# Attention over pooled keys, then an MLP: a waiting matmul group moved ahead of the keys' turn, a pooling sum moved from GpSimd to VectorE, and a transpose and three loads moved in time

## The chip, the cores and the metric

One Trainium2 chip; the program uses one core of it. The metric is the device time of one execution in microseconds. The kernel before took 284.84 us, the median of 3 runs (284.4 to 284.98).

## The reference

Shapes: q, k and v are [8, 8, 576, 64] (batch B, head, row, head size D) in float32, w_in is [512, 2048], w_out is [2048, 512].

```python
k_p = k.reshape(B, H, Sp, 8, D).mean(axis=3)      # Sp = 72 pooled keys
v_p = v.reshape(B, H, Sp, 8, D).mean(axis=3)
scores = scale * np.matmul(q, k_p.transpose(0, 1, 3, 2))
attn = softmax(scores)                             # with 1e-9 in the denominator
x = np.matmul(attn, v_p)                           # heads side by side: [4608, 512]
h = x @ w_in
out = (h - np.tanh(h)) @ w_out                     # [4608, 512]
```

Keys and values are pooled in eights, so that attention is small; the two matrix products of the MLP are most of the work.

## The kernel before

**Groups.** The 4608 rows are cut into nine groups of 512. Group b (0 to 7) holds the first 512 rows of batch b; the 64 left-over rows of every batch make up group 8, which runs last. The inputs of group 8 collect in the tile `xT_last`. Each group has an h stage (x times w_in, tanh, subtraction: `mlp_h` for group 0, L605; `h_pair`, L638, for the others) and an out stage (`mlp_o`, L611, for group 0; `product`, L683, for the others). Attention of the next batch is put between the matmuls of the out stage. The order of all instructions is written by hand: each engine runs its own in program order, and waits where it needs another engine's result or a free buffer.

**The out stage of group 0** (L1018 to L1083) is where the change lies. `mlp_o(0, tb, qd)` is four matmuls of 512 columns: row block tb (0 to 3), quarter qd of the hidden size. Quarter 0 needs the w_out rows of `w2_dmas[0]`, quarter 1 those of `w2_dmas[1]`, quarter 2 those of `w2_dmas[2]`, quarter 3 those of `w2_dmas[3]` (the loads `load_w2(0, 4)`, `(8, 4)`, `(4, 4)`, `(12, 4)`, L835 to L918). These loads turn float32 into float16 on their way and are issued by GpSimd; they run behind the loads of w_in, and on the same queue lie two loads of values of batch 1 (the second is `v1_last`, L917). Results go to PSUM banks 0 to 3.

**Batch 1 in that stage.** `pool_k(1, nc.gpsimd, last=nc.vector)` (L1018) adds eight rows of keys to one in three steps: 8 to 4 rows (L261), 4 to 2 (L267), 2 to 1 (L270, result `kd`). The first two run on GpSimd, the third, because of `last`, on VectorE. Behind it VectorE copies the queries of batch 1 from 16-bit storage (`q_bf`, L1020). `k_transpose(1)` (L360) turns `kd` on TensorE with five matmuls against the identity; VectorE copies the result out of PSUM with L342, L343 and L346 into `KB`. `q_pe_transpose` (L223) does the same for queries, four matmuls per pair of heads, copied out by ScalarE (L144). These, the scores (`scores_wide`, L406) and what follows take PSUM banks 4, 5, 6, 7 in turn (`ps_b1` over `Banks(4, 5, 6, 7)`, L1005): the keys' turn gets 4 and 5, query pairs 0 and 1 get 6 and 7, pairs 2 and 3 get 4 and 5 again. `pool_v1` (L300) sums the values of batch 1 on VectorE, tiles 2 and 3 of them after `v1_last` has landed. `av(1, blk)` (L540) makes block blk of x: matmuls L487, then on VectorE a reciprocal (L522) and a product (L523) into `x_sb`. `turn1(blk)` transposes it on TensorE (L566), and ScalarE copies it to `xT` (L573).

**Sums of weights.** The groups after 0 use sums and differences of quarters of w_out (`sum0` to `sum3`, L1006 to L1016, all by `w_sum`, L670, on VectorE with both inputs in SBUF). `sum1(4)` and `sum0(4)` (L1056, L1057) stand on VectorE between the products of `av(1, 1)` and `av(1, 2)`; `sum0(4)` reads the rows of `w2_dmas[3]`.

**Loads of batch 2.** `load_k(2)`, `load_v(2)`, `load_q(2)` (L1051 to L1053) are issued by SyncE, whose queue also carries every DMA transpose and the stores of group 0. `after(load_k(2), v1_last)` makes SyncE wait with them until `v1_last` has landed. When the keys of batch 2 have landed, GpSimd pools them (`pool_k(2, nc.gpsimd)`, L1077): L261 in two pieces of two and three tiles (`halves`), then L267 and L270.

**The left-over x of batch 0.** `av(0, 4)` (L995) writes it into the tile `x_end`, and `x_dma_transpose(0, 2)` (L996) has SyncE transpose it by DMA into `xT_last` (L557). The tile `P` holds the other blocks of x of batch 0 in `P[:, 0:4, :]` (L117), and is later written by `sum_p` (L651) in the h stage of group 1.

Of the kernel before, what the change touches and what calls it, by code (L numbers as in the profile page):

```python
# [43 lines left out]
def kernel(  # L44
# [57 lines left out]
    P = const.tile([128, NP, TG], BF16, name="P")  # L102
# [46 lines left out]
    def load_main(src, dst, b, t0, t1, eng=nc.sync):  # L149
        return eng.dma_start(out=dst[:, t0:t1, :], in_=src[b, 0:128, t0:t1, :])  # L150
# [7 lines left out]
    def load_dense(src, dst, b, eng=nc.sync):  # L158
        return eng.dma_start(
            out=dst[0 : NM * LO, NM, :], in_=src[b, 128:PR, :, :]  # L160
        )

    def load_k(b, eng=nc.sync):
        return [
            load_main(k_pairs, k_raw[b % 2], b, 0, NM, eng),
            load_dense(k_pairs, k_raw[b % 2], b, eng),
        ]
# [7 lines left out]
    def load_q_tail(b, t, eng):  # L175
        eng.dma_start(
            out=t[:QT, :, R, :], in_=q[b, :, QA:S, :].rearrange("h p d -> p h d")
        )

    def load_q(b, tail=True):  # L180
        if b not in q_raws:
            q_raws[b] = raw.tile([128, H, R + 1, D], FP32, name="q_raw", tag="q_raw")
        t = q_raws[b]
        nc.sync.dma_start(
            out=t[:, :, 0:R, :], in_=q[b, :, 0:QA, :].rearrange("h (p j) d -> p h j d", j=R)
        )
        if tail:
            load_q_tail(b, t, nc.sync)
# [62 lines left out]
    def halves(n, b):  # L251
        return ((0, n),) if b < 2 else ((0, n // 2), (n // 2, n))

    def pool_k(b, eng, t0=0, t1=NT, last=None):
        r = k_raw[b % 2].rearrange("p t (j d) -> p t j d", d=D)[:, t0:t1, :, :]
        if b not in kdups:
            kdups[b] = work.tile([128, NT, 2, D], BF16, name="kd", tag="kd", bufs=1)
        kd = kdups[b][:, t0:t1, :, :]
        n = t1 - t0
        for ta, tb in halves(n, b):  # L260
            eng.tensor_tensor(  # L261
                out=r[:, ta:tb, 0:4, :],
                in0=r[:, ta:tb, 0:4, :],
                in1=r[:, ta:tb, 4:8, :],
                op=ALU.add,
            )
        eng.tensor_tensor(  # L267
            out=r[:, :, 0:2, :], in0=r[:, :, 0:2, :], in1=r[:, :, 2:4, :], op=ALU.add
        )
        kd_done = (last or eng).tensor_tensor(  # L270
            out=kd,
            in0=r[:, :, 0:1, :].to_broadcast([128, n, 2, D]),
            in1=r[:, :, 1:2, :].to_broadcast([128, n, 2, D]),
            op=ALU.add,
        )
        return kd_done
# [63 lines left out]
    def kb_main(kb, ps, t0, t1, engs):  # L340
        kv = kb.rearrange("p (t x) -> p t x", x=KP)
        engs[0](out=kv[0:D, t0:t1, 0:G], in_=ps[0:D, :, 0:G])  # L342
        engs[1](out=kv[D:128, t0:t1, G:128], in_=ps[D:128, :, G:128])  # L343

    def kb_left(kb, ps, eng):
        eng(  # L346
            out=kb[D:128, :].rearrange("p (t x) -> p t x", x=KP)[:, :, 128 : 128 + LO],
            in_=ps[D:128, 0 : NM * LO].rearrange("p (x t) -> p t x", t=NM),
        )

    def turn_tile(dst, kd, t):
        nc.tensor.matmul(
            dst,
            lhsT=kd[:, t, :, :].rearrange("p a d -> p (a d)"),
            rhs=ident[:, :],
            start=True,
            stop=True,
        )

    def k_transpose(b, alloc, engs=(nc.vector.tensor_copy, nc.scalar.copy)):  # L360
        kd = kdups.pop(b)
        ps = alloc([128, NM, 128], FP32, "kT_ps")
        for t in range(NM):
            turn_tile(ps[:, t, :], kd, t)
        kb_main(KB[b % 2], ps, 0, NM, engs)
        ps = alloc([128, 128], FP32, "kT_ps")
        turn_tile(ps[:, :], kd, NM)
        kb_left(KB[b % 2], ps, nc.vector.tensor_copy)
# [131 lines left out]
    def av_half(b, blk, half, x_sb, alloc):  # L500
        ps = alloc([128, 4, D1], FP32, "x_ps")
        av_mms(b, blk, half, ps)
        rden = work.tile([128, 4, 1], FP32, name="rden", tag="rden", bufs=4)
        nc.vector.reciprocal(out=rden[:, :, :], in_=ps[:, :, D:D1])
        nc.vector.tensor_tensor(
            out=x_sb[:, half, :, :],
            in0=ps[:, :, 0:D],
            in1=rden[:, :, :].to_broadcast([128, 4, D]),
            op=ALU.mult,
        )  # L510

    def av_both(b, blk, x_sb):
        b0 = ps_a.ids[ps_a.n % len(ps_a.ids)]
        ps_a.n += 2
        ps = PS[:, b0 : b0 + 2, 0 : 4 * D1].rearrange("p k (h d) -> p k h d", d=D1)
        if b < 2:
            for half in range(2):
                av_mms(b, blk, half, ps[:, half, :, :])
        else:
            head_av_mms(b, blk, ps)  # L520
        rden = work.tile([128, 2, 4, 1], FP32, name="rden2", tag="rden2")
        nc.vector.reciprocal(out=rden[:, :, :, :], in_=ps[:, :, :, D:D1])  # L522
        nc.vector.tensor_tensor(  # L523
            out=x_sb[:, :, :, :],
            in0=ps[:, :, :, 0:D],
            in1=rden[:, :, :, :].to_broadcast([128, 2, 4, D]),
            op=ALU.mult,
        )

    x_pairs = {}  # L530

    def x_block(b, blk):
        if blk == 4:
            x_pairs[b, 2] = work.tile([128, 2, 4, D], BF16, name="x_end", tag="x_end", bufs=1)
            return x_pairs[b, 2]
        if blk % 2 == 0:
            x_pairs[b, blk // 2] = work.tile([128, 2, 2, 4, D], BF16, name="x_sb", tag="x_sb")
        return x_pairs[b, blk // 2][:, blk % 2]

    def av(b, blk, alloc, both):  # L540
        x_sb = x_block(b, blk)
        if both:
            av_both(b, blk, x_sb)
        else:
            for half in range(2):
                av_half(b, blk, half, x_sb, alloc)
        return x_sb

    def x_dma_transpose(b, n):
        if n < 2:  # L550
            nc.sync.dma_start_transpose(
                out=xT[b % 2][:, 2 * n : 2 * n + 2, :, :].rearrange("p k f c -> p (k f) c"),
                in_=x_pairs.pop((b, n)).rearrange("p k a h d -> p (k a h d)"),
            )
        else:
            c = (b % 2) * QT
            nc.sync.dma_start_transpose(  # L557
                out=xT_last[:, b // 2, :, c : c + QT],
                in_=x_pairs.pop((b, 2))[128 - QT : 128].rearrange("p a h d -> p (a h d)"),
            )  # L560
# [44 lines left out]
    def mlp_h(g, i, gts, pool):  # L605
        mlp_h_mms(g, i, 0, NFB, pool)
        mlp_h_act(i, gts)
# [3 lines left out]
    def mlp_o(g, tb, qd, gts):  # L611
        if qd == 0:
            o_tiles[tb] = bank((1, 2, 3, 0)[tb], [128, DM])
        o_ps = o_tiles[tb]
        i0 = W2_ORDER[qd]
        for i in range(i0, i0 + 4):
            nc.tensor.matmul(  # L617
                o_ps[:, :],
                lhsT=gts[i][:, tb * 128 : (tb + 1) * 128],
                rhs=w2b[:, i, :],  # L620
                start=(i == 0),
                stop=(i == NHID - 1),
            )
        if qd == 3:
            nc.scalar.copy(out=O[:, tb, :], in_=o_ps[:, :])
# [127 lines left out]
    w2_dmas = []  # L753
# [13 lines left out]
    def after(lds, dep):  # L767
        for ld in lds:
            tc.add_manual_dep(
                ld.ins,  # L770
                dep.ins.name,
                mybir.DependencyInfo(mybir.DependencyClass.Sync, mybir.DependencyReason.DATA),
            )
# [143 lines left out]
    v1_last = load_main(v_pairs, v_raw[1], 1, 2, 4, nc.gpsimd)  # L917
    load_w2(12, 4)  # L918
    gts = []
# [67 lines left out]
    for i in range(5, NHID):  # L987
        mlp_h(0, i, gts, bank(i % 5 if i > 5 else 5, [128, TG]))
        if i == 7:
            q_pe_tail(0)  # L990
        if i == 9:
            scores_tail(0)
        if i == 11:
            ps_a.n = 0
            av(0, 4, ps_any, True)  # L995
            x_dma_transpose(0, 2)  # L996
    def turn1(blk):
        x_pe_transpose(1, blk, x_pairs[1, blk // 2][:, blk % 2])

# [24 lines left out]
    mlp_o(0, 0, 0, gts)  # L1024
    mlp_o(0, 1, 0, gts)
    mlp_o(0, 2, 0, gts)
    k_transpose(1, ps_any, (nc.vector.tensor_copy, nc.vector.tensor_copy))
    q_pe_transpose(1, (0, 1), "act")
    mlp_o(0, 3, 0, gts)
    sum1(0)  # L1030
    sum2(0)
    sum0(0)
# [15 lines left out]
    mlp_o(0, 1, 2, gts)  # L1048
    mlp_o(0, 2, 2, gts)
    ps_a.n = 0  # L1050
    after(load_k(2), v1_last)  # L1051
    load_v(2)
    load_q(2)  # L1053
    av(1, 0, ps_any, True)
    av(1, 1, ps_any, True)
    sum1(4)  # L1056
# [131 lines left out]
```

## Time and profile before

| what | value |
|---|---|
| median of the runs | 284.84 us |
| the profiled execution's own time | 284.74 us |
| its span, first to last instruction | 282.9 us |
| busy: TensorE / VectorE / ScalarE / GpSimd | 274.3 / 222.6 / 155.2 / 118.5 us |
| h stage of group 1 begins (first matmul of L630) | 52.67 us |
| moved by DMA | 49.82 MB, mean 176 GB/s |

The span begins with the first instruction. A time such as "35.65" is microseconds from there. In a row of the timeline the first number is the start, the second the length; rows of equal kind are merged and counted (x4), and the brackets give the engine's idle time ahead of the row and what ended it. PE is TensorE, PEld its weight loads, DVE VectorE, ACT ScalarE, POOL GpSimd, SP SyncE. Matmul rows contain the pipeline's depth: a matmul of 512 columns is listed with 379 ns, while the next starts some 216 ns after it. A DMA's time to landing runs from its issue to its completion.

### The profile page before, as it was taken

To read this page: it belongs to the slowest core of one execution; us is meant where nothing else is said; L and a number is where in the kernel's file an instruction comes from. 1 tells how busy PE (TensorE), PEld (TensorE's weight loads), DVE (VectorE), ACT (ScalarE), POOL (GpSimd) and SP (SyncE) were. 2 spreads that over 40 slices of the span, in tenths; PEclk is the share of its full clock that TensorE was granted. 3 is DMA by queue.
4 is the path that set the end of the run, shared out by engine and by line. 5 is a ranking of instruction groups with operands and counts; after the bars stand their busy time and mean duration, and the time that the engine had idled before them with its cause. 6 is when DMAs were issued, how large, how long until landed. Compare 5 with 4: busy or idle time off the path is not lost.

```text
span 282.9 us, 5497 instructions
## 1 busy us (share of the span) xinstructions
PE 274.3 (97%) x2174; PEld 180.8 (64%) x2174; DVE 222.6 (79%) x336; ACT 155.2 (55%) x209; POOL 118.5 (42%) x132
## 2 busy tenths in 40 slices
PE   7999899999999999999999999999999999999994
PEld 3574355645974588458944895489547954884583
DVE  6658687999957996699759985999599749936983
ACT  4767373697337653766276628571867056216610
POOL 8844601992596039802980199019900200010000
PEclk9999999999999999999999999999999999999999
DMA  7999998999958894779588949796640440011014
GB/s 250 237 212 270 231 229 256 333 203 256 273 94 214 240 289 88 181 253 331 89 177 267 324 76 156 235 340 123 134 143 1 80 154 2 0 73 79 0 39 111
DMA packets 66491, 49.82 MB, mean 176 GB/s; under 512 B 42104, under 2 KB 55944, under 8 KB 66466
## 3 DMA queue, kind: packets, MB, share of 16 engines
q1 hardware_dynamic: 55538, 33.87, 47.5%
q0 software_dynamic: 8736, 13.77, 20.1%
q10 hardware_dynamic: 2192, 1.84, 2.2%
q8 instruction: 17, 0.28, 0.4%
q14 instruction: 8, 0.07, 0.1%
HBM read 36.70 MB, written 9.44 MB: 163 GB/s over the span
## 4 chain that ended last, share of the span: by engine, by line
PE 83%; DMA 10%; POOL 3%; DVE 1%; issue 1%; SPq 0%; POOLq 0%; DVEq 0%
PE PS L630 39%; PE PS L687 33%; DMA w1b<-in_moe_w_in_dram 5%; PE PS L617 4%; DMA k_raw<-in_k_dram 3%; PE PS L446 3%; PE PS L472 2%; DMA xT<-x_sb 2%; POOL k_raw L261 1%; DVE x_sb L523 1%; PE PS L487 1%; POOL v_raw L827 1%; POOL k_raw L267 1%; PE PS L398 1%; PE PS L566 0%
## 5 line engine op out<-in xcount | busy, mean ns | idle before, releaser
L630 PE MATMUL PS<-xT,w1b 128*128 128x512 bf16 (+1 forms) x504 | 98.1, 355 | 0.5 <-DMA xT<-x_sb 0.5
L644 DVE TENSOR_TENSOR Gt<-PS,TS 128x1024 bf16<-128x1024 f32 x56 | 68.3, 1220 | 32.1 <-ACT TS L643 32.1
L630 PEld LDWEIGHTS <-w1b 128*128 128x128 f16 x576 | 56.4, 98 | 53.5 <-issue 0.7
L643 ACT ACTIVATE TS<-PS 128x1024 f32<-128x1024 f32 x56 | 57.3, 1024 | 30.3 <-PE PS L630 28.2
L731 POOL TENSOR_TENSOR m<-O,m 128x512 f32<-128x512 f32 x6 | 7.6, 1260 | 75.6 <-ACT m L729 62.2
L687 PE MATMUL PS<-w2s,Dg 128*128 128x256 f16 x256 | 30.2, 272 | 0.0
L261 POOL TENSOR_TENSOR k_raw<-k_raw 128x512 f32<-128x512 f32 (+2 forms) x13 | 21.3, 1651 | 17.6 <-DMA k_raw<-in_k_dram 17.6
L467 ACT ACTIVATE E<-PS 72x1024 bf16<-72x1024 f32 (+1 forms) x30 | 26.0, 929 | 4.0 <-PE PS L446 3.7
L687 PEld LDWEIGHTS <-Gt 128*128 128x128 bf16 x256 | 23.6, 98 | 6.8 <-issue 2.3
L687 PEld LDWEIGHTS <-P 128*128 128x128 bf16 x256 | 24.5, 98 | 3.0
L687 PEld LDWEIGHTS <-Dg 128*128 128x128 bf16 x256 | 24.6, 98 | 2.8
L652 DVE TENSOR_TENSOR P<-Gt 128x1024 bf16<-128x1024 bf16 x32 | 22.0, 686 | 0.5
L703 POOL DMA_DIRECT2D out_dram<-O x14 | 7.7, 554 | 31.7 <-DVE O L741 29.5
L738 ACT COPY m<-PS 128x512 f32<-128x512 f32 x8 | 4.7, 585 | 29.6 <-PE PS L687 29.6
L662 DVE TENSOR_TENSOR Dg<-Gt 128x1024 bf16<-128x1024 bf16 x32 | 20.4, 682 | 0.0
L523 DVE TENSOR_TENSOR x_sb<-PS,rden 128x512 bf16<-128x512 f32 x28 | 19.4, 691 | 1.0
L282 POOL TENSOR_TENSOR v_raw<-v_raw 128x512 f32<-128x512 f32 (+1 forms) x12 | 19.2, 1616 | 0.0
L687 PE MATMUL PS<-w2s,Gt 128*128 128x256 f16 x128 | 16.4, 273 | 0.0
L687 PE MATMUL PS<-w2b,P 128*128 128x256 f16 x128 | 16.3, 273 | 0.0
L687 PE MATMUL PS<-w2b,Gt 128*128 128x256 f16 x128 | 16.3, 272 | 0.0
L687 PE MATMUL PS<-w2s,Q 128*128 128x256 f16 x128 | 16.3, 272 | 0.0
L1150 ACT COPY O<-PS 128x512 f32<-128x512 f32 x7 | 4.1, 585 | 21.9 <-PE PS L687 21.9
(123 smaller groups left out, 400.5 us busy)
## 6 DMA issues: line engine op xcount, KB each, us to landing
k_raw<-in_k_dram SPq DMA_DIRECT2D x7, 1024.0 KB, 6.1
out_dram<-O POOLq DMA_DIRECT2D x14, 512.0 KB, 4.4
v_raw<-in_v_dram SPq DMA_DIRECT2D x6, 1024.0 KB, 8.1
q_raw<-in_q_dram SPq DMA_DIRECT2D x6, 1024.0 KB, 11.4
w1b<-in_moe_w_in_dram POOLq DMA_DIRECT2D x4, 512.0 KB, 13.9
w2b<-in_moe_w_out_dram POOLq DMA_DIRECT2D x4, 512.0 KB, 21.6
v_raw<-in_v_dram POOLq DMA_DIRECT2D x2, 512.0 KB, 21.9
out_dram<-O SPq DMA_DIRECT2D x2, 512.0 KB, 6.3
```

Source lines behind the costliest of these rows:

```text
L261: eng.tensor_tensor(out=r[:, ta:tb, 0:4, :], in0=r[:, ta:tb, 0:4, :], in1=r[:, ta:tb, 4:8, :], op=ALU.add,)
L282: eng.tensor_tensor(out=r[:, ta:tb, 0:4, :], in0=r[:, ta:tb, 0:4, :], in1=r[:, ta:tb, 4:8, :], op=ALU.add,)
L446: nc.tensor.matmul(dst, lhsT=kv[a * D : (a + 1) * D, m, :], rhs=rhs, start=True, stop=True,)
L467: nc.scalar.activation(out=e, in_=ps, func=ACT.Exp, scale=SCALE)
L523: nc.vector.tensor_tensor(out=x_sb[:, :, :, :], in0=ps[:, :, :, 0:D], in1=rden[:, :, :, :].to_broadcast([128, 2, 4, D]), op=ALU.mult,)
L617: nc.tensor.matmul(o_ps[:, :], lhsT=gts[i][:, tb * 128 : (tb + 1) * 128], rhs=w2b[:, i, :], start=(i == 0), stop=(i == NHID - 1),)
L630: nc.tensor.matmul(dst[:, t0 * 128 : t1 * 128], lhsT=w1b[:, fb, i * 128 : (i + 1) * 128], rhs=x[:, t0:t1, fb, :], start=(fb == 0), stop=(f ...
L643: nc.scalar.activation(out=t2, in_=PS[:, b0 : b0 + 2, :], func=ACT.Tanh)
L644: nc.vector.tensor_sub(out=Gt[:, p, :, :], in0=PS[:, b0 : b0 + 2, :], in1=t2)
L652: nc.vector.tensor_tensor(out=P[:, a:b, :], in0=Gt[:, a:b, 0, :], in1=Gt[:, a:b, 1, :], op=ALU.add)
L662: return nc.vector.tensor_tensor(out=Dg[:, a:b, :, :], in0=Gt[:, a:b, :, 0:HT], in1=Gt[:, a:b, :, HT:TG], op=ALU.subtract,)
L687: nc.tensor.matmul(part(g, bk, tt), lhsT=lhs(k, slice(tt * 128, (tt + 1) * 128)), rhs=rhs[:, k, :], start=(first and k == 0 and (tt == 0 o ...
```

## The change

Five edits, all in or near the out stage of group 0:

1. In `pool_k`, the second sum (L267) also goes to the engine given as `last`. Only the call for batch 1 gives one, so that there VectorE does the second and the third sum, and GpSimd the first alone.
2. `mlp_o(0, 3, 0)` is moved from behind `q_pe_transpose(1, (0, 1))` to ahead of `k_transpose(1)`.
3. The left-over x of batch 0 is put into `P[:, 4, :]` instead of the tile `x_end`.
4. `x_dma_transpose(0, 2)` is moved from behind `av(0, 4)` to behind `load_q(2)` in SyncE's queue.
5. `load_k(2)` waits for `w2_dmas[2]` instead of `v1_last`; `load_v(2)` and `load_q(2)` follow it in the same queue.

```diff
         (pool_k)
-        eng.tensor_tensor(
+        (last or eng).tensor_tensor(
             out=r[:, :, 0:2, :], in0=r[:, :, 0:2, :], in1=r[:, :, 2:4, :], op=ALU.add
         )
...
     def x_block(b, blk):
+        if b == 0:
+            x_pairs[b, 2] = P[:, 4, :].rearrange("p (s h d) -> p s h d", s=2, h=4)
+            return x_pairs[b, 2]
...
             av(0, 4, ps_any, True)
-            x_dma_transpose(0, 2)
...
     mlp_o(0, 2, 0, gts)
+    mlp_o(0, 3, 0, gts)
     k_transpose(1, ps_any, (nc.vector.tensor_copy, nc.vector.tensor_copy))
     q_pe_transpose(1, (0, 1), "act")
-    mlp_o(0, 3, 0, gts)
...
     ps_a.n = 0
-    after(load_k(2), v1_last)
+    after(load_k(2), w2_dmas[2])
     load_v(2)
     load_q(2)
+    x_dma_transpose(0, 2)
     av(1, 0, ps_any, True)
     av(1, 1, ps_any, True)
```

## The prediction

> **What bounds the kernel now.** First the page's busy times and the shares of the chain that ended last:
>
> ```profile
> PE 274.3 (97%) x2174; PEld 180.8 (64%) x2174; DVE 222.6 (79%) x336; ACT 155.2 (55%) x209; POOL 118.5 (42%) x132
> ...
> PE 83%; DMA 10%; POOL 3%; DVE 1%; issue 1%; SPq 0%; POOLq 0%; DVEq 0%
> ```
>
> TensorE has 8.6 us without work in a span of 282.9, so an edit pays only where TensorE stands. The waits between 28 and 68 us show one place in the change's reach; here is that stretch in TensorE's timeline, then the chain of waits behind it:
>
> ```profile
> 31.48 2.75 PE L617 MATMUL PS<-w2b,Gt 128*128 128x512 f16 x12
> 35.65 0.45 PE L352 MATMUL PS<-ident,kd 128*128 128x128 bf16 x5 [1.41 <-DVE kd L270]
> 35.98 0.62 PE L228 MATMUL PS<-ident,q_bf 128*128 128x128 bf16 x8
> 36.44 1.03 PE L617 MATMUL PS<-w2b,Gt 128*128 128x512 f16 x4
> 37.30 0.61 PE L228 MATMUL PS<-ident,q_bf 128*128 128x128 bf16 x8
> ```
>
> ```profile
> 20.24 9.84 DMA k_raw<-in_k_dram
> 30.22 2.91 POOL k_raw L261
> 33.20 1.53 POOL k_raw L267
> 34.76 0.84 DVE kd L270
> 35.65 0.45 PE PS L352 x5
> ```
>
> The fourth L617 group (36.44) waits for nothing, yet stands behind the keys' turn. Matmuls of 512 columns issue 0.216 us apart, so TensorE could go on at 34.07, and stands 1.58 us in issue time (1.41 by listed ends).
>
> Two more views limit what can be won. DMAs to landing, for `w2_dmas[1]` (issued 12.62), `w2_dmas[2]` (20.04), `v1_last` (23.11), `w2_dmas[3]` (25.82):
>
> ```profile
> w2b<-in_moe_w_out_dram POOLq DMA_DIRECT2D x1, 512.0 KB, 25.5
> ...
> w2b<-in_moe_w_out_dram POOLq DMA_DIRECT2D x1, 512.0 KB, 21.6
> ...
> v_raw<-in_v_dram POOLq DMA_DIRECT2D x1, 512.0 KB, 19.9
> ...
> w2b<-in_moe_w_out_dram POOLq DMA_DIRECT2D x1, 512.0 KB, 19.7
> ```
>
> They land at 38.1, 41.6, 43.0 and 45.5. The first user of `w2_dmas[1]` starts at 38.20 where it could at 38.08: TensorE is already 0.12 us ahead of the weights. And GpSimd against VectorE:
>
> ```profile
> 48.72 3.24 POOL L261 TENSOR_TENSOR k_raw<-k_raw 128x512 f32<-128x512 f32 x2 [13.99 <-DMA k_raw<-in_k_dram]
> 52.04 1.87 POOL L267 TENSOR_TENSOR k_raw<-k_raw 128x640 f32<-128x640 f32 x1
> ```
>
> ```profile
> 47.78 1.28 DVE L670 TENSOR_TENSOR w2s<-w2b 128x1024 f16<-128x1024 f16 x2
> ...
> 51.08 1.43 DVE L670 TENSOR_TENSOR w2s<-w2b 128x1024 f16<-128x1024 f16 x1
> ...
> 53.27 1.19 DVE L670 TENSOR_TENSOR w2s<-w2b 128x1024 f16<-128x1024 f16 x1
> ```
>
> A weight sum takes 0.68 us, but 1.43 and 1.19 beside GpSimd. Both end 0.55 us after GpSimd's instruction of the moment (51.96 and 53.91): VectorE waits out the whole instruction. The pair at 47.78 (`sum1(4)`, `sum0(4)`) escapes, because GpSimd comes only at 48.72.
>
> [...] the products L523 (one input in PSUM) keep 0.69 us beside GpSimd. [...] the trace's 128x640 sum L270 has 826.
>
> **The change part by part.** The sum is against the profiled execution: 282.9 span plus 1.84 around it, 284.74; the median is 284.84.
>
> *Second sum on VectorE.* GpSimd loses L267 (1.52 us). VectorE gains one of 640 float32 elements: 0.83. VectorE's last subtraction ends at 33.00, GpSimd's first sum at 33.12, so the new sum runs 33.16 to 33.99, and `kd` is ready at 34.86 instead of 35.59: 0.73 sooner. Nothing new waits behind it: the copies L1020 stood behind the same wait. They follow 0.73 sooner (their queries came 21.7 us after 11.74, at 33.4).
>
> *`mlp_o(0, 3, 0)` ahead.* Same four matmuls, 4 x 0.216 = 0.86, from 34.07 to 34.93. Its bank's last reader ended at 33.00. `kd` comes at 34.86 plus 0.06 handover: the wait is gone, almost to the point. Either edit alone would leave some: 0.73 or 0.86 of 1.58.
> What is late next: the matmuls were cover for banks. Turn and first queries take 0.79 us as before, to 35.72. Queries 2 and 3 need bank 4, read by L342 and L343: VectorE is free at 35.45, 0.45 + 0.40 later it is 36.31, plus 0.06. TensorE waits 0.65 us, to 36.37. Then 0.45 + 0.11 + 0.22 (from the starts 37.30, 37.75, 37.86) to 37.15 for the first quarter-1 matmul, against 38.20.
> Gain 1.58 - 0.65 + 0.12 = **1.05 us**, if the weights have landed by 37.15. Scores and their exponentials after that find banks free (ScalarE's copies of queries end by about 38.2).
>
> *Transpose moved.* Its issue (1.28 us of SyncE at 30.07) leaves, and so does its traffic at 34 to 37.6. The table by microsecond from 34 (last columns: clock, DMA share, GB/s):
>
> ```profile
> 35.00:36.00 1.00, 0.35 (x6) 0.30 (x7) 1.00 (x3) 0.00 (x0) 0.00 (x0) 1.00 1.25 87
> 36.00:37.00 1.00, 1.00 (x13) 0.73 (x12) 0.99 (x4) 0.58 (x2) 0.00 (x0) 1.00 0.96 207
> ...
> 38.00:39.00 1.00, 1.00 (x6) 0.38 (x4) 0.81 (x2) 1.00 (x4) 0.00 (x0) 1.00 1.26 222
> ```
>
> In 35 to 36 the weights' queue starts 29 packets, in 38 to 39 it starts 199, and 93 in 36 to 37: (170 + 106)/199 = 1.4 us lost; a little is the mixture of packet sizes. I take 1.2 (bounds: 0, if the stall has another cause, and 2.3: `w2_dmas[1]` came 4.7 us after the load ahead of it, its fellow `w2_dmas[3]` 2.5 after `v1_last`, and the difference also holds other traffic). So all later landings come 1.2 sooner: 36.9, 40.4, 41.8, 44.3. That meets 37.15, and `v1_last`'s values are in `VB` 1.94 later, at 43.8, before `av(1, 0)` at 44.43.
> In its new place it goes past the six load issues on SyncE and stands ahead of the store, issued at 50.91, that waits for ScalarE: SyncE idles there from 46.7. Its packets run behind the queries' loads, which landed at 57.0 and now come sooner. The new reader of `P[:, 4, :]` must be done before the sum that rewrites it, past 64 us; behind that sum stand the subtractions L644, but there are some 8 us of slack. Cost 0. Writing to `P` instead of `x_end` costs 0: same product, 0.69 us, no user there.
>
> *Loads sooner.* Batch 2 loads issue at 40.4 instead of 43.0. Their first packets came 1.9 us after the issue, so at 42.3, when the weights' last packets are still due. Before, the keys met that tail too (0.2 us of it); [...] the keys land not 2.6 but about 1.2 sooner: 48.5 to 47.3, and GpSimd's first sum wants to start at 48.72 - 1.2 = **47.5**. `w2_dmas[3]` [...] from 44.3 at worst to 45.9; its user comes at 47.32 - 1.05 = 46.27. Cost 0 (0 to 0.3).
>
> *The point that decides.* `sum1(4)` and `sum0(4)` now start at 46.73 and 47.33 (1.05 sooner). GpSimd at 47.5 comes just after the second has started, and waits for it, as before. Then the rest keeps its pattern, and from 51.62 on TensorE's rows simply move. The 0.48 us wait for `xT` at 83.09 stays.
> Sum: 284.74 - 1.05 = **283.69**.
>
> **Rivals.**
> *A, as above:* 283.7 (283.2 to 284.2).
> *B, GpSimd gets in between the two sums* (start 46.73 to 47.33, keys 0.2 to 0.8 us sooner than I take): `sum0(4)` waits for the first piece of L261 (1.26 us, fastest row): ends 1.13 later. The reciprocal and product of `av(1, 2)` stand behind it, and `turn1(2)` on TensorE has no slack (its input was just in time). Net +0.08: 284.8.
> *C, slower:* GpSimd starts ahead of `sum1(4)`, that is before 46.73, from keys 2.0 us sooner on. With 46.4: first piece to 47.66, `sum1(4)` to 48.21, second piece (1.80) to about 49.95, `sum0(4)` to 50.5 instead of 48.0. `turn1(2)` stands 2.4 us: net +1.35, 286.1. For it: the loads are issued 2.6 us sooner, and the bound of 2.3. Against it: the tail of the weights.
> *D, the weights come no sooner* (the stall isn't the transpose's): quarter 1 waits to 38.1, and the gain is 0.1: 284.6. For it: the transpose moves only 64 KB (64 rows of 512 values of 2 bytes). Against it: the stall lies inside their time.
>
> **Numbers.** A 0.55, B 0.14, C 0.21, D 0.10. The likeliest gives 283.7. The range starts at 283.2, and reaches past D and B to 285.8, into C's lower part; about 2 in 10 is left out. Cases of both signs: A's own range is 283.2 to 284.2. A measurement of this kernel tells about 0.2% (0.57 us) from no change. Faster: A and a little of D, 0.57; same: B and the rest of D, 0.21; slower: C, 0.22.
>
> **What would show it.** L352 starts near 34.95 with no wait for `kd`, and a new wait of 0.65 stands before the second L228 group. Quarter 1 starts near 37.15; near 38.1 is D. The table has no slice near 87 GB/s around 35. `sum1(4)` and `sum0(4)` with 0.68 each are A; one of them over 1.2 is B or C, with an L566 row behind a wait for L523. The h stage of group 1 starts at 51.6 (A), 52.7 (B), 54.0 (C). I am wrong if the stall of 35 to 36.3 is not the transpose's, or if the keys' landing moves with their issue.

## The result, and the profile after

The kernel after took 286.13 us, the median of 18 runs (284.55 to 288.01). The kernel before, in runs taken between them on the same chip, took 284.72 us (18 runs). The ratio is 1.0065 [1.0041, 1.0088] (in brackets here and below: the 95% interval): the change makes the kernel slower, by 0.65%, where the forecast was 1.05 us (0.37%) faster. Ratios compare mean times and leave out three single slow runs (291.42 us of before here, 287.92 and 289.60 us in the third and fourth experiment); the medians here lie 0.50% apart. The time lies outside the range, 0.3 us above its end, and the case that came true is C. The profiled execution took 287.29 us, with a span of 285.6.

The page after, busy times and shares of the chain that ended last:

```profile
PE 275.4 (96%) x2172; PEld 181.8 (64%) x2174; DVE 226.4 (79%) x337; ACT 155.6 (54%) x209; POOL 117.6 (41%) x131
...
PE 89%; DVE 4%; DMA 4%; issue 1%; POOL 1%; DVEq 0%; POOLq 0%
```

DMA's share of the chain fell from 10% to 4% and GpSimd's from 3% to 1%, as intended: the long chain of loads and sums behind `kd` is gone. VectorE's share rose from 1% to 4%; the two weight sums of the new wait are 1.3 points of it (3.66 us), the rest is spread over many short pieces. TensorE's idle time went from 8.6 us of the span to 10.2. TensorE's timeline after shows the old wait gone and the new one there (line numbers past the edits are three higher: L617 is now L620, L566 is L569, L630 is L633, L670 is L673):

```profile
31.61 3.62 PE L620 MATMUL PS<-w2b,Gt 128*128 128x512 f16 x16
35.06 0.44 PE L352 MATMUL PS<-ident,kd 128*128 128x128 bf16 x5
...
36.40 0.61 PE L228 MATMUL PS<-ident,q_bf 128*128 128x128 bf16 x8 [0.45 <-DVE KB L343]
...
37.17 1.03 PE L620 MATMUL PS<-w2b,Gt 128*128 128x512 f16 x4
...
51.39 0.40 PE L569 MATMUL PS<-ident,x_sb 128*128 128x128 bf16 x4 [2.30 <-DVE x_sb L523]
```

Up to 37.17 everything stands where the forecast put it. The second sum takes 0.81 us on VectorE (L267 at 33.05); the forecast's 0.83 is what the sum L270 of the same 128x640 took before, 826 ns. Sixteen matmuls run through, the keys' turn starts at 35.06 with no wait (forecast 34.95), a wait for bank 4 takes its place, and quarter 1 starts at 37.17 (forecast 37.15, before 38.20). Then, at 51.39, 2.30 us are lost for the product of `av(1, 2)`. The chain of waits after tells what was in front of that product:

```profile
46.84 3.66 DVE w2s L673 x2
...
50.64 0.70 DVE x_sb L523
51.35 0.05 issue
51.39 0.40 PE PS L569 x4
```

The two weight sums `sum1(4)` and `sum0(4)`, 1.28 us together before, take 3.74 us, and 3.66 of that is on the path. VectorE's timeline after lists the pair, and GpSimd's names the reason:

```profile
46.75 3.74 DVE L673 TENSOR_TENSOR w2s<-w2b 128x1024 f16<-128x1024 f16 x2
```

```profile
46.46 3.48 POOL L261 TENSOR_TENSOR k_raw<-k_raw 128x512 f32<-128x512 f32 x2 [14.51 <-DMA k_raw<-in_k_dram]
```

GpSimd's first sum starts at 46.46, 2.26 us sooner than before (48.72), and 0.29 us ahead of `sum1(4)` (46.75). One by one: GpSimd's pieces run from 46.46 to 47.73 and from 47.69 to 49.94; `sum1(4)` ends at 48.27, `sum0(4)` at 50.49, each about 0.55 us after a piece. This is the pattern of case C.

GpSimd came so soon because its keys did. DMAs to landing after, for `w2_dmas[1]` (issued at 12.87), `v1_last` (22.66), `w2_dmas[3]` (26.44) and the keys of batch 2 (39.61):

```profile
w2b<-in_moe_w_out_dram POOLq DMA_DIRECT2D x1, 512.0 KB, 22.9
...
v_raw<-in_v_dram POOLq DMA_DIRECT2D x1, 512.0 KB, 18.1
...
w2b<-in_moe_w_out_dram POOLq DMA_DIRECT2D x1, 512.0 KB, 16.8
...
k_raw<-in_k_dram SPq DMA_DIRECT2D x1, 1024.0 KB, 6.7
```

They land at 35.8, 40.8, 43.3 and 46.3. Each is 2.2 to 2.4 us sooner than in the first profile of before, where the forecast took 1.2.

A second loss shows only in the table by microsecond after (the third number from the end is TensorE's granted clock):

```profile
52.00:53.00 1.00, 1.00 (x10) 0.70 (x8) 1.00 (x2) 0.72 (x2) 1.00 (x1) 0.77 2.00 190
53.00:54.00 1.00, 1.00 (x9) 0.73 (x8) 1.00 (x2) 0.76 (x2) 1.00 (x2) 0.50 0.58 66
...
56.00:57.00 1.00, 1.00 (x11) 0.89 (x10) 1.00 (x1) 0.06 (x1) 1.00 (x1) 1.00 0.38 82
```

From 52.5 on, after the wait, TensorE runs at half its clock for some 3.4 us. That costs up to 1.7 us (an estimate, half of 3.4): the h stage of group 1 begins at 55.23, where case C said 54.0. Of the 18 runs, 7 took 287.29 to 288.01 us, with a mean clock of 0.990 to 0.993 over the run; the other 11 took 284.55 to 286.28, with 0.996 to 1.0. The medians of the two sets, 287.70 and 285.95, lie 1.75 apart.

### The profile page after: what moved, and what is told of

The parts are those of the page before. It is cut to its first block, busy times and chain, and to the rows that moved or that the text cites. A ratio compares the mean times of both kernels' runs of the same rounds, so it can differ in the third digit from the quotient of the medians.

```text
span 285.6 us, 5496 instructions
## 1 busy us (share of the span) xinstructions
PE 275.4 (96%) x2172; PEld 181.8 (64%) x2174; DVE 226.4 (79%) x337; ACT 155.6 (54%) x209; POOL 117.6 (41%) x131
## 4 chain that ended last, share of the span: by engine, by line
PE 89%; DVE 4%; DMA 4%; issue 1%; POOL 1%; DVEq 0%; POOLq 0%
PE PS L633 39%; PE PS L690 33%; PE PS L591 5%; PE PS L620 4%; PE PS L446 3%; PE PS L472 2%; DMA v_raw<-in_v_dram 2%; DMA xT<-x_sb 2%; DVE x_sb L523 1%; DVE w2s L673 1%; PE PS L398 1%; PE PS L487 1%; PE PS L877 0%; DVE rden L522 0%; PE PS L944 0%
## 5 line engine op out<-in xcount | busy, mean ns | idle before, releaser
L633 PE MATMUL PS<-xT,w1b 128*128 128x512 bf16 (+1 forms) x504 | 98.5, 356 | 0.1
L633 PEld LDWEIGHTS <-w1b 128*128 128x128 f16 x576 | 56.6, 98 | 53.6 <-issue 0.8
L620 PE MATMUL PS<-w2b,Gt 128*128 128x512 f16 x64 | 16.2, 395 | 0.0
```

Source lines behind the costliest of these rows:

```text
L620: nc.tensor.matmul(o_ps[:, :], lhsT=gts[i][:, tb * 128 : (tb + 1) * 128], rhs=w2b[:, i, :], start=(i == 0), stop=(i == NHID - 1),)
L633: nc.tensor.matmul(dst[:, t0 * 128 : t1 * 128], lhsT=w1b[:, fb, i * 128 : (i + 1) * 128], rhs=x[:, t0:t1, fb, :], start=(fb == 0), stop=(f ...
```

## The experiments

**The theories.** *Lock:* GpSimd's sooner start on the keys of batch 2 makes both weight sums wait, and that is the loss. *Rival, keys' side:* the rewrite around the keys' turn (edits 1 and 2) costs elsewhere. *Rival, loads:* the earlier loads delay others. Each kernel below was run beside the kernel before, whose median was 284.47 for the first four experiments (75 runs), 284.36 for the next four (35 runs) and 284.12 for the last three (35 runs).

### The two sums moved to where GpSimd is idle

```diff
     (the kernel after; new place: right behind pool_v1(2, 4))
+    sum1(4)
+    sum0(4)
...
     av(1, 1, ps_any, True)
-    sum1(4)
-    sum0(4)
```

> The changed kernel, with sum1(4) and sum0(4) moved ahead of av(1, 0) on VectorE, where it stood idle from 42.8 to 45.1 us; nothing else. Lock theory (the two sums wait out GpSimd's first sums of keys, and TensorE's 2.3 us wait for x_sb of block 2 comes from that): the wait is gone, the h stage of group 1 starts at 51.6 instead of 55.2, no slice of the clock at half, 283.6 us, 1.1 below the kernel before. Rival 1 (the sooner loads themselves cost the time, by contention among transfers): the wait stays within 0.5 us of its size, 286. Rival 2 (the clock drop has another cause): the wait goes, but runs still split in two groups 1.7 us apart.

Measured: 284.19 us (283.55 to 284.56, 22 runs), ratio to before 0.9987 [0.9972, 1.0002]. VectorE's timeline of this kernel, the two sums and the product that was late:

```profile
42.88 1.31 DVE L673 TENSOR_TENSOR w2s<-w2b 128x1024 f16<-128x1024 f16 x2
...
48.42 0.69 DVE L523 TENSOR_TENSOR x_sb<-PS,rden 128x512 bf16<-128x512 f32 x1
```

The sums take their 1.31 us again, and the product starts at 48.42 instead of 50.64, while GpSimd is as early as in the kernel after (46.61). The h stage of group 1 begins at 51.89, near the place that case A gave it (51.6), and no stretch of it runs at half the clock. So the wait behind the lock is the loss of the kernel after: ratio 1.0065 with it, 0.9987 without. The rival on the loads falls, since they are as early here. The 283.6 us that were expected did not come: with the wait gone, no gain of 1.05 us appears.

### The loads wait for `v1_last` again

```diff
-    after(load_k(2), w2_dmas[2])
+    after(load_k(2), v1_last)
```

> The changed kernel with edit 5 undone: load_k(2) waits for v1_last again. Rival 1 (the sooner loads are to blame): 283.7, no wait for x_sb of block 2. Lock theory: [...] v1_last itself came 2.2 us sooner, at 40.8; so GpSimd starts at 46.7 to 47.2 instead of 46.5, still against the sums at 46.75 and 47.35: one or both wait, TensorE stands 1.1 to 2.3 us, 284.8 to 286.2.

Measured: 284.76 us (283.70 to 287.90, 22 runs), ratio 1.0016 [0.9991, 1.0040]: inconclusive as a time, clear as a profile. The keys are issued 1.4 us later (41.01), but land only 0.74 later (47.06); GpSimd starts at 47.20, after the first sum (46.88) and ahead of the second. TensorE's timeline:

```profile
50.14 0.40 PE L569 MATMUL PS<-ident,x_sb 128*128 128x128 bf16 x4 [0.92 <-DVE x_sb L523]
```

One sum waits, and TensorE stands 0.92 us: case B. Of its runs 15 lie below 285.1, the profiled one with its 0.92 us among them (284.80), four at 285.8 to 286.2, and three at 287.7 to 287.9, with a mean clock of 0.990 to 0.994. The last three look like the kernel after; no profile was taken of them. Edit 5 is thus not needed for a collision: without it, one sum is still caught in the profile. But the three profiles of this study in which both sums are caught all have edit 5.

### Only the transpose moved

The kernel before with edits 3 and 4 alone.

```diff
     def x_block(b, blk):
+        if b == 0:
+            x_pairs[b, 2] = P[:, 4, :].rearrange("p (s h d) -> p s h d", s=2, h=4)
+            return x_pairs[b, 2]
...
             av(0, 4, ps_any, True)
-            x_dma_transpose(0, 2)
...
     load_q(2)
+    x_dma_transpose(0, 2)
```

> The kernel before with edits 3 and 4 alone: the left-over x in P, its DMA transpose behind load_q(2). TensorE's rows up to 45 us are unchanged, with the 1.4 us wait for kd. Lock theory: w2_dmas[1] lands some 2 us sooner (near 36), v1_last near 41, so load_k(2) is issued 2 us sooner and GpSimd starts near 46.8, while sum1(4) still stands at 47.8: sum1(4) and sum0(4) take 1.2 us or more each, turn1(2) waits 1.5 to 2.4 us, 286.3 to 287.2, slower than before with none of the four other effects. If the transpose has no part in the weights' landing: w2_dmas[1] stays at 38.1 and the time at 284.7.

Measured: 284.19 us (283.21 to 287.92, 22 runs), ratio 0.9981 [0.9963, 0.9999]. The expectation missed. The weights came as expected (`w2_dmas[1]` at 35.95, `v1_last` at 40.98) and the keys were issued at 41.05, but took 7.1 us to land, at 48.12. In VectorE's timeline of this kernel the sums are over before GpSimd starts, at 48.26:

```profile
46.55 1.28 DVE L673 TENSOR_TENSOR w2s<-w2b 128x1024 f16<-128x1024 f16 x2
```

TensorE was itself sooner than I had assumed, since the wait for `kd` was small, and took the sums out of GpSimd's way. Two of the 22 runs (286.62 and 287.92) look as if they had the collision; no profile was taken of them. Why these keys took 7.1 us stays open. The same load after the same wait took 6.0 in the experiment before, 5.6 in a later one with the late transpose, and in three profiles of the kernel before 5.55, 5.57 and 7.45: its landing moves by more than a microsecond from one execution to the next. This kernel is not slower than the one before: its interval lies just below 1.

### TensorE kept busy during the wait

Eleven matmuls of zeros, whose result nothing reads, put into the kernel after where TensorE stands.

```diff
+    warm_pe(11, b0=1)
     turn1(2)
```

> The changed kernel with eleven matmuls of zeros (512 columns, 2.4 us) on TensorE between av(1, 3) and turn1(2), in the place of the wait; their result is not used. If the halved clock after the wait (0.50 for 3.4 us in the profile) comes from TensorE standing idle: no run under 0.998, all runs near 286.0, and the two groups of runs become one. If the clock drop has another cause: runs still split, some near 287.7.

Measured: 285.73 us (285.21 to 289.60; 20 of 22 runs at most 286.56), ratio 1.0035 [1.0019, 1.0050]. The collision is unchanged (two sums in 3.84 us). TensorE's timeline (the zeros lie in the tile `xT_last`, so the view names that), and a line of the table by microsecond:

```profile
49.15 2.54 PE L780 MATMUL PS<-xT_last 128*128 128x512 bf16 x11
51.71 0.40 PE L569 MATMUL PS<-ident,x_sb 128*128 128x128 bf16 x4
```

```profile
53.00:54.00 1.00, 1.00 (x13) 0.67 (x11) 1.00 (x1) 1.00 (x2) 1.00 (x2) 1.00 1.99 117
```

The turn is as late as in the kernel after, but the clock stays at 1.00, and the group of runs near 287.7 is gone. Four of the 22 runs have a mean clock of 0.997, a little under the 0.998 that was named, but so have runs of the kernel before; none is near the 0.990 to 0.993 of the slower set. The cause of the two runs above 287 (0.997 and 0.999) is open. So the halved clock is a consequence of TensorE standing, a second price on the same wait, and not a cause of its own. The h stage begins at 54.24, close to case C's 54.0.

### The kernel before, profiled again

Unchanged, two more executions, to see how fixed the waits are on which the forecast was built.

> The kernel before, unchanged, for a second profile. In the five profiles of the changed kernel and its variants, w1_dmas[1] landed at 18.5 us and the keys of batch 1 at 28.0 and 28.9, against 19.75 and 30.1 in the profile that the prediction was made from; none of the edits acts so early. If that profile was an unusual execution: keys near 29.0 here, kd near 34.5, and TensorE waits for kd 0.2 to 0.4 us instead of 1.41. If one of the edits moves it: keys at 30.1 and the wait of 1.4 again.

> The kernel before once more, a third profile, with the same two expectations: keys near 29.0 and a wait for kd of 0.2 to 0.4 us if the first profile was an unusual execution, keys at 30.1 and 1.4 us if an edit moves them.

Measured: 284.05 and 286.12 us. TensorE's timeline of the first, and its chain of waits:

```profile
35.03 0.45 PE L352 MATMUL PS<-ident,kd 128*128 128x128 bf16 x5 [0.34 <-DVE kd L270]
```

```profile
6.61 12.21 DMA w1b<-in_moe_w_in_dram
...
19.32 10.14 DMA k_raw<-in_k_dram
29.46 0.02 issue
```

The wait for `kd` is 0.34 us here and 0.20 in the other; in the profile of the prediction it was 1.41. The chain says where the difference starts: the keys of batch 1 are issued when the second load of w_in lands, and that was at 18.8 in both of these, against 19.75 in the first profile. In all other profiles of this study that load landed between 18.4 and 18.8. The keys then landed 0.62 us later (30.08 against 29.46), and the first quarter-0 matmul came 0.45 us sooner (31.48 against 31.93); together that is the 1.07 us between 1.41 and 0.34. So of three executions of this kernel, that with 1.41 us was the odd one. Why that load was late once, the profiles do not settle. The second execution has other waits instead: 0.46 us for `w2_dmas[1]` at 37.89 and 0.85 us for `Gt` at 69.02. Its keys of batch 2 landed only at 50.36, where the two other profiles of this kernel have 48.27 and 48.59.

### Only the keys' side changed

The kernel before with edits 1 and 2 alone.

```diff
-        eng.tensor_tensor(
+        (last or eng).tensor_tensor(
...
+    mlp_o(0, 3, 0, gts)
     k_transpose(1, ps_any, (nc.vector.tensor_copy, nc.vector.tensor_copy))
     q_pe_transpose(1, (0, 1), "act")
-    mlp_o(0, 3, 0, gts)
```

> The kernel before with edits 1 and 2 alone: second sum on VectorE, mlp_o(0, 3, 0) ahead of the keys' turn. The transpose stays at 30 us and the loads wait for v1_last. If the weights' landing is the next limit, as case D of the prediction has it: w2_dmas[1] lands near 37.5 to 38.2, TensorE waits for it at the first quarter-1 matmul, the gain is 0 to 0.3 us, 284.2 to 284.6. If the two edits are worth their 1.05 us by themselves: 283.4.

Measured: 284.59 us (283.81 to 287.93, 14 runs), ratio 1.0006 [0.9981, 1.0032]. No gain and no loss that can be told from noise, and a loss of 0.65% lies outside the interval: the rival on the keys' side falls too. One of the 14 runs, 287.93 us with a clock of 0.991, looks like the slower set of the kernel after; it was not profiled. The expected limit, the weights, was met only nearly: `w2_dmas[1]` landed at 37.22, and quarter 1 began at 37.30 without a wait for it. The wait for `kd` is gone, and in TensorE's timeline its successor is there:

```profile
36.53 0.61 PE L228 MATMUL PS<-ident,q_bf 128*128 128x128 bf16 x8 [0.45 <-DVE KB L343]
```

The stretch from the first matmul of `mlp_o(0, 0, 0)` to the first of quarter 1 makes the trade plain. It lasts 5.56 or 5.57 us in all seven profiles with edit 2 and the copies out of the bank on VectorE, edit 1 or not (37.17 - 31.61 in the kernel after). In the kernel before it lasted 6.72 (38.20 - 31.48) in the first profile, 5.70 and 6.01 in the two others, where `w2_dmas[1]` landed only at 37.59 and 37.85, just ahead of quarter 1 (37.63 and 37.89), and 5.33 and 5.47 with the late transpose alone, in the third and the next experiment. The ready unit takes away a wait that is usually 0.2 to 0.3 us, and takes the cover from another of 0.45.

### The late transpose and the early sums, without edits 1, 2 and 5

The third experiment, with the sums moved as in the first:

```diff
+    sum1(4)
+    sum0(4)
...
     av(1, 1, ps_any, True)
-    sum1(4)
-    sum0(4)
```

> The kernel before with edits 3 and 4 (left-over x in P, late transpose) and sum1(4), sum0(4) ahead of av(1, 0); edits 1, 2 and 5 are left out. If the late transpose is the part that pays, and the only thing it needs is that the two sums keep out of GpSimd's way: 283.6 to 284.0, at or below the kernel e1_sums_early, with no run over 285. If edits 1 and 2 pay as well: slower than e1_sums_early by 0.5 us or more.

Measured: 283.97 us (283.23 to 284.60, 22 runs), ratio 0.9978 [0.9965, 0.9991]. With the third experiment, which it builds on, this is the version whose interval lies below 1: the late transpose pays about 0.2% if edits 1 and 2 are left out. That those two take something away is not shown: the first experiment's 0.9987 [0.9972, 1.0002] overlaps. This version keeps the sooner weights, has nothing that GpSimd could hold up (no run above 284.6, where the third experiment had two above 286), and waits 0.28 us for `kd`. Some of what it wins by 51.46 (h stage, against 52.09 in the second profile of before) is lost again to a wait of 0.50 us for `Gt` at 67.37.

### The second sum of keys back on GpSimd

The first experiment without edit 1.

```diff
-        (last or eng).tensor_tensor(
+        eng.tensor_tensor(
```

> The kernel e1_sums_early with edit 1 undone: the second sum of keys on GpSimd again. In the profile of e1_sums_early VectorE's last subtraction ends at 33.3 us, and the second sum can only follow it (33.30 to 34.12), kd 34.98; in e6_late_transpose_early_sums GpSimd has it done at 33.65, and kd at 34.51. If edit 1 gives nothing once the keys come at 28 to 29 us: kd 0.4 us sooner, the wait for L343 down from 0.45 to below 0.2, 283.8 to 284.0. If edit 1 is worth its 0.7 us: slower than e1_sums_early, 284.7.

Measured: 284.26 us (283.64 to 284.51, 22 runs), ratio 0.9995 [0.9984, 1.0006], against 0.9987 [0.9972, 1.0002] with edit 1. Nothing measurable. `kd` was ready at 34.71, ahead of the turn at 35.15, so that edit 1 had only slack to win. I had expected a shorter bank wait and was wrong: it stays at 0.45, because VectorE's copy L342 waits for the turn (idle 0.19 us ahead of it) and not for VectorE.

### The bank's second copy on ScalarE

The late transpose, `mlp_o(0, 3, 0)` ahead, `sum1(4)`, `sum0(4)` and `sum3(4)` early, and L343 given to ScalarE to shorten the bank wait.

```diff
-    k_transpose(1, ps_any, (nc.vector.tensor_copy, nc.vector.tensor_copy))
+    k_transpose(1, ps_any, (nc.vector.tensor_copy, nc.scalar.copy))
```

> The version that the runs point to: edits 2, 3 and 4; edits 1 and 5 left out; sum1(4), sum0(4) and sum3(4) ahead of av(1, 0); the copy L343 of the keys' turn on ScalarE beside L342 on VectorE. Expected: no wait for kd, none over 0.2 us for the bank, none for x_sb, h stage of group 1 at 51.1 to 51.4, 283.4 to 283.8, all runs below 284.5, against 284.4 of the kernel before. If the time is set elsewhere (the weights' landing): 284.0, as e6_late_transpose_early_sums.

Measured: 284.84 us (284.31 to 285.43, 14 runs), ratio 1.0015 [0.9998, 1.0033]: a failure. ScalarE's timeline of this kernel:

```profile
36.07 0.34 ACT L343 CAST KB<-PS 64x224 bf16<-64x224 f32 x1 [3.62 <-DVE KB L342]
```

ScalarE's copy waited for VectorE's copy L342, which ended at 35.98: the two ran in turn, and the bank wait stayed (0.46 us). Why they ran in turn is not shown; they read and write different partitions, 0 to 63 and 64 to 127. ScalarE's copies of queries came later for it, and TensorE waits another 0.21 us for them. The stretch to quarter 1 lasts 6.12 us, against 5.47 in the experiment with the late transpose and the early sums. Since this kernel also differs from that one in `mlp_o(0, 3, 0)` and `sum3(4)`, the rest of its 284.84 us is not taken apart.

### The kernel after, profiled again

> The changed kernel, unchanged, for a second profile. Lock theory: sum1(4) and sum0(4) again over 1.2 us each, GpSimd's first sum of keys begins before 46.8, TensorE waits 2 us or more for x_sb of block 2, the clock at half or full after it. If the collision were one of this execution alone: GpSimd begins after 47.3 and the wait is absent.

Measured: 287.32 us, clock 0.991. GpSimd starts at 46.43, the sums take 3.77 us from 46.69, TensorE stands 2.33 us, and the clock falls to 0.50 for some 3.4 us. The collision is not an accident of one profile.

## Why the prediction was wrong

**The point that decides was the right one.** What settles the result is when GpSimd starts on the keys of batch 2, against the start of `sum1(4)`. These are all profiles in which the two sums stand in their old place:

| kernel | `sum1(4)` starts | GpSimd starts | two sums take | TensorE waits |
|---|---|---|---|---|
| before, first profile | 47.78 | 48.72 | 1.28 | none |
| before, second | 47.21 | 48.40 | 1.28 | none |
| before, third | 47.47 | 50.49 | 1.28 | none |
| keys' side alone | 46.88 | 48.21 | 1.28 | none |
| transpose alone | 46.55 | 48.26 | 1.28 | none |
| after, loads wait for `v1_last` | 46.88 | 47.20 | 2.36 | 0.92 |
| after | 46.75 | 46.46 | 3.74 | 2.30 |
| after, second | 46.69 | 46.43 | 3.77 | 2.33 |
| after, with matmuls of zeros | 46.97 | 46.77 | 3.84 | filled |

Where GpSimd starts after the second sum's start, no sum waits; between the two starts, one does; ahead of the first, both: 1.28, 2.36 and 3.74 to 3.84 us for the same two instructions. The views show the waits and their order; what inside the chip makes VectorE wait for GpSimd they do not show.

**The step that failed: "I take 1.2", for how much sooner all later loads land without the transpose.** The keys came 2.27 us sooner, not 1.2, and GpSimd started at 46.46, not 47.5, ahead of `sum1(4)`, which started where it was forecast (46.75, forecast 46.73). My own threshold for C was 2.0. The working was sound in kind. The slice at 35 us, with 87 GB/s before, looks like this after:

```profile
35.00:36.00 1.00, 0.95 (x15) 0.77 (x13) 0.89 (x4) 0.24 (x1) 0.00 (x0) 1.00 1.13 283
```

The weights also come sooner with edits 3 and 4 alone (third experiment). So the stall was the transpose's, and case D is out. The size was read from packets started in three slices of one profile. The better measure was the one I had named as the upper bound (4.7 less 2.5, which is 2.2 and not 2.3). From the landing of the load ahead of it in the queue to that of `w2_dmas[1]`, four profiles with the transpose at 30 us have 4.00 to 4.68 us (mean 4.28), nine with the late transpose have 2.53 to 2.72 (mean 2.65). The transpose costs the queue 1.6 us on average, and against the first profile of before 2.0; the other 0.3 is that this execution ran sooner.

**How the landing moves was right only in part.** The forecast gave edit 5 nothing: the keys would end behind the weights' tail, however soon they were issued. That was my estimate; no view of before showed what holds the keys there. In the first profile of before and in the kernel after they do land 3.06 us behind `w2_dmas[3]`, though issued 3.4 us sooner (39.6 against 43.0). But with the late transpose, which brings the weights to 43.3 to 43.6 in all nine profiles, the keys landed at 46.78, 46.97, 47.06 and 48.12 where they waited for `v1_last`, and at 46.29 to 46.63 in the five profiles with edit 5. So edit 5 brought them forward too, by 0.8 us on the mean, and always to 3.0 to 3.1 us behind the weights. GpSimd starts some 0.14 us after them, so from 46.8 to 48.1 it would have come behind the start of `sum1(4)`, at 46.75, and so caught one sum or none. That landing also varies by itself, from 48.27 to 50.36 in three profiles of the kernel before, while the forecast put only 0.77 us between case A (47.5) and case C (46.73).

**The base of the gain failed too: the wait of 1.58 us for `kd`.** It was in the profile, but not in the kernel: two more profiles list 0.34 and 0.20 us where the first had 1.41. What takes its place, the wait for bank 4, was forecast well (0.65 in issue time; listed 0.45 or 0.46 in every profile with edit 2), and it is no smaller than the usual wait. So edits 1 and 2 bring nothing measurable (1.0006), and with C avoided the gain of 1.05 did not appear (0.9987, with an interval that reaches to 0.28% below before, where 1.05 us are 0.37%). A wait in one execution was taken for a property of the program; the times of three runs, which agreed within 0.6 us, gave no hint of it.

**Case C was priced well.** A wait of 2.4 us was forecast, 2.30 and 2.33 came; 286.1 us were given, 286.13 is the median. Part of that agreement is luck: the price was set against a gain of 1.05 us that no version shows, and what makes the sum agree is that the kernel after is a mixture. Its 11 runs at full clock have a median of 285.95, 1.2 above before, less than the wait. Waits later in the program may absorb a part: 0.48 us for `xT` at 83.09 in the first profile of before and 0.55 at 84.41 in the third, but none in the second, and none after. The remainder is not accounted for. The 7 others carry the halved clock, which no step foresaw.

**Costs put at nothing held.** The late transpose was not waited for (it landed at 56.2), `w2_dmas[3]` was early (landed at 43.3), and TensorE stood for neither. No wait in the profile after stems from the left-over x in `P`.

## What to carry to other kernels

A transfer that ends sooner is a new start time for the engine that waits for it (here keys 2.27 us and GpSimd 2.26 us sooner): before moving a load, list what runs on the other engines at its new landing, and put sums that no one waits for where GpSimd is idle (1.31 us for the two there, 3.74 beside GpSimd's own sums). A wait fed by a long chain of DMAs should be seen in more than one execution before an edit is built on it. A wait taken from one unit can have been the cover of the next one (here 0.45 us, for bank 4), so look for the bank or buffer that this unit's time had hidden. Where the good case and the bad one are parted by the order of two starts, ask how far each start varies between executions: a margin smaller than that is no margin.

## What the runs showed of the hardware that was not expected

A wait of 2.30 us on TensorE (2.33 in the second profile) was followed by some 3.4 us at half the granted clock, in both profiles of the kernel after. The mean clock, 0.990 to 0.993, points to the same in 7 of its 18 timed runs, and to none in the other 11 (0.996 to 1.0); what decides which runs are hit is not shown. With matmuls of zeros in the place of the wait the clock stayed at 1.00. Waits of 1.41 us (first profile of before) and 0.92 us (second experiment) were not followed by half the clock.

A DMA transpose of 64 KB held back another queue's loads by 1.6 us (means of 4.28 and 2.65 us). At the 222 GB/s of the slice at 38 us before, 64 KB would take 0.3 us (an estimate from these two figures), so its size alone does not explain it. The move of the left-over x to `P` (edit 3) went with it in every run.
